# 64x128 array tiles with a row tile per token group, in place of 64x64 tiles with copied operands, in a convolution and feed-forward kernel

## Chip, cores, metric

One core of one Trainium2 chip. The metric is device time in microseconds of a whole execution. Every kernel was run several times next to the kernel before on the same chip. Engines: PE is TensorE (PEld its weight loads), ACT ScalarE, DVE VectorE, POOL GpSimd, SP the queue that issues most transfers.

## The reference

A causal convolution of 7 taps along the sequence, with one softmax-normalised set of taps for each of 8 heads, feeds a two-layer network with an ELU between the layers:

```python
# x (8, 4096, 192), weight (8, 7), w_in (192, 2048), w_out (2048, 192)
w = softmax(weight)                                   # per head
a[b, s, h*24 + g] = sum_k w[h, k] * x[b, s + k - 6, h*24 + g]
h = a @ w_in                                          # 32768 tokens
g = where(h > 0, h, exp(min(h, 0)) - 1)
out = g @ w_out                                       # (32768, 192) f32
```

## The kernel before

Work goes in 32 *supersteps* of 1,024 tokens, each of two groups of 512. A superstep has 16 *pairs*; a pair makes 128 of the 2,048 features for all its tokens:

- PE: H = w_in^T a, contracted in three chunks of 64 rows. The chunks are 64 rows so that two row tiles of the array can work at once (in the trace the four matmuls of a round start within about 10 ns).
- ACT takes exp of H (two instructions of 128x512), POOL clamps it, DVE combines it with H to g (written as `gT`).
- H lives in a ring of three PSUM slots; a slot is free again when DVE has read it. A convolution takes a slot of the same ring.
- PE: the output matmuls ("rounds") of an earlier superstep stand between the H blocks.

```python
LAG = -4                                   # output of superstep t starts 4 pairs before its last H
HALF_STEPS = (10, 9, 9, 9, 9, 9, 9)        # output rounds behind each H block, 64 per half
CONV_AT = ((7, 2, 0), (15, 2, 1))          # pair, supersteps ahead, group
X_AT = (1, 5, 13)                          # pairs at which POOL issues loads of x
...
# H: four 64x64 tiles at once, r = row tile (a feature block of 64), c = token group
for j in range(3):
    for r in range(2):
        f = 2 * q + r
        for c in range(2):
            pe.matmul(H[HP*c : HP*(c+1), k % 3, GS*r : GS*(r+1)],
                      w_in[HP*r : HP*(r+1), j, HP*f : HP*(f+1)],
                      att[HP*r : HP*(r+1), s % 2, j, c, :],      # att and w_in stand twice, in
                      tile_position=(HP*r, HP*c), ...)           # partitions 0-63 and 64-127
...
# output: g = row tile and token group, c = half of a block of 128 tokens
for r in range(r0, r1):
    f, kb = divmod(r, 2) if half == 0 else divmod(r, NF)[::-1]
    W(s_tt, 2 * NQ * t + f + 1)
    for g in range(2):
        for c in range(2):
            t0 = P * b + HP * c
            pe.matmul(ops[HP*c : HP*(c+1), g, D*kb : D*(kb+1)],
                      gT[HP*g : HP*(g+1), t % NG3, f, t0 : t0+HP],
                      w_out[HP*g : HP*(g+1), f, :],              # w_out stands twice too
                      tile_position=(HP*g, HP*c), ...)
```

## Time and profile before

| kernel before | |
|---|---|
| time, median of 4 | 850.47 us (847.81 to 851.45) |
| first H matmul / first output round | 34.45 / 55.95 us |
| superstep, mean | 25.1 us |
| PE instructions | 25,088 matmuls and as many weight loads |

The superstep in this document is the mean distance, in the trace, between ACT's copies of every second output half (30 distances, from the first half of superstep 0 to that of superstep 30).

The queues of the transfers, from the same page: name and kind, packets, MB, share of 16 engines.

```profile
q1 hardware_dynamic: 68016, 69.30, 26.1%
q0 software_dynamic: 40944, 15.72, 17.1%
q8 instruction: 196, 3.21, 1.6%
```

The page gives the queue q8 as one of instructions. 3.21 MB over 2 x 25,088 PE instructions are 64 bytes each, so I take this queue for PE's own stream; all its 196 packets have 16,384 bytes, which is 256 instructions.

PE in the timeline of the kernel before, around a convolution (start, length, engine, what, count, idle before):

```profile
386.12 0.84 PE L392 MATMUL H<-att,w_in 64*64 64x512 bf16 x12
386.79 0.91 PE L414 MATMUL ops<-w_out,gT 64*64 64x192 f16 x36
387.54 0.82 PE L392 MATMUL H<-att,w_in 64*64 64x512 bf16 x12
388.18 0.91 PE L414 MATMUL ops<-w_out,gT 64*64 64x192 f16 x36
389.24 0.67 PE L370 MATMUL H<-Tm,xg 128*24 128x24 bf16 x40
390.53 0.84 PE L392 MATMUL H<-att,w_in 64*64 64x512 bf16 x12 [0.62 <-DVE gT L333]
```

The last column shows the stall of the ring: H behind the convolution waits 0.62 us for DVE. Starts count here, not lengths, since matmuls overlap in the records (the H block at 387.54 has a length of 0.82 us, and the next rounds start within it): from 387.54 to 388.18 an H block takes 0.64 us, and from 386.79 to 387.54 nine rounds take 0.75 us.

### The profile page before, as it was taken

What the parts mean: (1) busy time and instruction counts of PE and PEld (TensorE: products, weight loads), DVE (VectorE), ACT (ScalarE), POOL (GpSimd) and SP (SyncE); (2) the same over time, 40 slices, a digit from 0 to 9 for tenths busy, and PEclk for the clock granted to TensorE, in tenths of its full rate; (3) what the DMA queues carried; (4) which work ended last, traced back from release to release, by engine and by line L of the source; (5) the groups of instructions that cost most, each with busy time, mean ns of one, the idle gap of its engine ahead of it and who ended that gap; (6) DMA issues with size and microseconds to landing.
All of it is one profiled execution on the core that took longest, in us unless ns stands there. A gap on an engine that the chain in (4) does not pass through costs nothing.

```text
span 849.9 us, 54707 instructions
## 1 busy us (share of the span) xinstructions
PE 752.5 (89%) x25088; PEld 560.4 (66%) x25088; DVE 643.3 (76%) x1031; ACT 650.5 (77%) x1156; POOL 662.8 (78%) x1115
## 2 busy tenths in 40 slices
PE   0279999889999999989999989999999999999997
PEld 0147667667766666766766766767766766677776
DVE  1277878777878878778777877878787887888894
ACT  1278888778878878878888868888787887888884
POOL 3378888778788788878788868788778878877883
PEclk9999999999999999999999999999999999999999
DMA  7774453444453444444335444344445434443211
GB/s 121 131 148 114 105 121 94 94 99 111 106 123 90 109 94 110 115 106 111 102 80 117 112 101 110 96 93 112 106 106 122 100 91 103 111 115 94 91 41 59
DMA packets 109190, 88.51 MB, mean 104 GB/s; under 512 B 46432, under 2 KB 95584, under 8 KB 108896
## 3 DMA queue, kind: packets, MB, share of 16 engines
q1 hardware_dynamic: 68016, 69.30, 26.1%
q0 software_dynamic: 40944, 15.72, 17.1%
q8 instruction: 196, 3.21, 1.6%
q14 instruction: 34, 0.28, 0.1%
HBM read 56.89 MB, written 42.24 MB: 117 GB/s over the span
## 4 chain that ended last, share of the span: by engine, by line
PE 35%; POOL 26%; DVE 17%; ACT 9%; issue 9%; DMA 3%; SPq 0%; POOLq 0%; ACTq 0%
POOL E L248 20%; PE H L392 19%; DVE gT L333 17%; PE ops L414 16%; ACT E L294 6%; POOL xg L198 5%; ACT osb L271 3%; DMA conv_slots<-csb 1%; DMA conv_band<-wprb 1%; DMA att<-conv_slots 1%; PE H L370 1%; DMA Tm<-conv_band 0%; SPq L475 0%; DMA wq<-in_weight_dram 0%; ACT csb L283 0%
## 5 line engine op out<-in xcount | busy, mean ns | idle before, releaser
L333 DVE SCALAR_TENSOR_TENSOR gT<-E,H 128x512 f16<-128x512 f32 x1024 | 640.0, 682 | 191.0 <-POOL E L248 182.1
L248 POOL TENSOR_SCALAR E<-E 128x512 f32<-128x512 f32 x1024 | 602.4, 614 | 148.1 <-ACT E L294 142.7
L294 ACT ACTIVATE E<-H 128x512 f32<-128x512 f32 x1024 | 546.6, 605 | 138.4 <-PE H L392 138.1
L392 PE MATMUL H<-att,w_in 64*64 64x512 bf16 x6144 | 429.7, 381 | 57.7 <-DVE gT L333 38.3
L414 PEld LDWEIGHTS ops<-w_out,gT 64*64 64x64 f16 x16384 | 377.9, 107 | 90.1 <-issue 9.5
L414 PE MATMUL ops<-w_out,gT 64*64 64x192 f16 x16384 | 422.5, 243 | 7.5 <-issue 6.4
L392 PEld LDWEIGHTS H<-att,w_in 64*64 64x64 bf16 x6144 | 165.9, 107 | 154.2 <-DVE gT L333 63.5
L283 ACT ACTIVATE csb<-H 128x1024 bf16<-128x1024 f32 x64 | 65.5, 1024 | 47.1 <-PE H L370 47.1
L370 PE MATMUL H<-Tm,xg 128*24 128x122 bf16 (+1 forms) x2560 | 43.2, 212 | 28.3 <-DMA Tm<-conv_band 15.2
L370 PEld LDWEIGHTS H<-Tm,xg 128*24 128x24 bf16 x2560 | 33.9, 93 | 41.2 <-DMA Tm<-conv_band 15.2
L198 POOL DMA_DIRECT2D xg<-in_x_dram x64 | 53.0, 830 | 10.2 <-DMA Tm<-conv_band 10.2
L271 ACT ACTIVATE osb<-ops 128x768 f32<-128x768 f32 x64 | 52.3, 817 | 8.4 <-PE ops L414 8.4
L235 POOL DMA_DIRECT2D w_out<-in_moe_w_out_dram x1 | 1.1, 1102 | 15.4 <-DMA att<-conv_slots 15.4
L207 POOL DMA_DIRECT2D xg<-in_x_dram x8 | 4.8, 604 | 0.3 <-issue 0.3
L217 POOL DMA_DIRECT2D w_in<-in_moe_w_in_dram x6 | 3.5, 606 | 0.3 <-PE H L370 0.3
L206 POOL MEMSET xg<- 6x192 bf16 x8 | 2.0, 247 | 0.3 <-POOLq L512 0.3
L326 DVE MEMSET H<- 128x2048 f32 x1 | 1.8, 1765 | 0.4 <-issue 0.4
L307 DVE TENSOR_REDUCE wmx<-wq 128x8 f32<-128x56 f32 x1 | 0.2, 213 | 2.2 <-DMA wq<-in_weight_dram 2.2
L260 ACT ACT_TABLE_LOAD x1 | 1.3, 1283 | 0.7 <-PEq L512 0.7
L264 ACT ACTIVATE wex<-wq 128x56 f32<-128x56 f32 x1 | 0.2, 249 | 1.7 <-DVE wq L309 1.7
L305 DVE MEMSET Tm<- 128x544 uint32 x1 | 0.5, 512 | 0.9 <-PEq L512 0.9
L316 DVE TENSOR_REDUCE wsum<-wex 128x8 f32<-128x56 f32 x1 | 0.2, 211 | 0.3 <-ACT wex L264 0.3
(9 smaller groups left out, 1.5 us busy)
## 6 DMA issues: line engine op xcount, KB each, us to landing
att<-conv_slots SPq DMA_DIRECT2D x192, 128.0 KB
out_dram<-osb SPq DMA_DIRECT2D x128, 192.0 KB, 3.3
conv_slots<-csb SPq DMA_DIRECT2D x64, 256.0 KB, 2.2
xg<-in_x_dram POOLq DMA_DIRECT2D x40, 192.0 KB, 3.7
xg<-in_x_dram POOLq DMA_DIRECT2D x24, 240.0 KB, 5.3
w_in<-in_moe_w_in_dram POOLq DMA_DIRECT2D x6, 128.0 KB, 5.6
w_in<-w_in SPq DMA_DIRECT2D x2, 384.0 KB, 5.3
w_out<-in_moe_w_out_dram POOLq DMA_DIRECT2D x1, 768.0 KB, 8.4
```

Of the source, the lines that this page charges most:

```text
L198: g.dma_start(xg[:, s % NXB, w0:w1, :], src).then_inc(s_x[s % NXB], 16)
L206: g.memset(xg[0:PAD, b, 0, :], 0.0).then_inc(s_z)
L207: g.dma_start(xg[PAD:P, b, 0, :], x_flat[t0 : t0 + P - PAD, :]).then_inc(s_x[b], 16)
L217: g.dma_start(w_in[0:HP, j, FH * k : FH * (k + 1)], bass.AP(tensor=moe_w_in.tensor, offset=8 * j * FF + FH * k, ap=[[CPH * FF, HEADS], [FF ...
L248: g.tensor_scalar(out=E[:, n % NE, u, :], in0=E[:, n % NE, u, :], scalar1=1.0, scalar2=0.0, op0=ALU.min, op1=ALU.max,).then_inc(s_clp)
L271: a.activation(osb[:, b, :, :, :].rearrange("p g k d -> p g (k d)"), ops[:, :, 0 : 2 * D], ACT.Copy,).then_inc(s_oev)
L283: a.activation(csb[:, m % 4, :, :], H[:, slot_of_conv[m] % 3, :].rearrange("p (b t) -> p b t", b=2), ACT.Copy,).then_inc(s_ce)
L294: a.activation(E[:, n % NE, u, :], H[:, k, GS * u : GS * (u + 1)], ACT.Exp).then_inc(s_exp)
L333: v.scalar_tensor_tensor(out=gT[:, s % NG3, 2 * q + u, :], in0=E[:, n % NE, u, :], scalar=1.0, in1=H[:, slot_of_pair[n] % 3, GS * u : GS * ...
L370: ins = pe.matmul(H[SLOT * q : SLOT * q + CPH, k % 3, GS * hb + o : GS * hb + o + nc_], xg[:, s % NXB, w, CPH * h : CPH * (h + 1)], Tm[:, ...
L392: ins = pe.matmul(H[HP * c : HP * (c + 1), k % 3, GS * r : GS * (r + 1)], w_in[HP * r : HP * (r + 1), j, HP * f : HP * (f + 1)], att[HP * ...
L414: ins = pe.matmul(ops[HP * c : HP * (c + 1), g, D * kb : D * (kb + 1)], gT[HP * g : HP * (g + 1), t % NG3, f, t0 : t0 + HP], w_out[HP * g ...
```

## The change

The intent: tiles of 64 rows and 128 columns. Row tile r works on token group r, so the convolution's output needs no second copy in the other 64 partitions, and w_out needs none either. In the output, the two tiles swap token groups after half of the rounds, so that by design they never accumulate into the same token group's half of `ops` at the same time. PE gets half the matmuls, each twice as wide. The order of work changes with it.

```diff
-LAG = -4
-HALF_STEPS = (10, 9, 9, 9, 9, 9, 9)
-CONV_AT = ((7, 2, 0), (15, 2, 1))
-X_AT = (1, 5, 13)
+LAG = -1
+WARM = (20, 18)                            # dummy matmuls ahead of the convolution and of H
+HALF_STEPS = (9, 9, 7, 7, 11, 11, 10)
+CONV_AT = ((4, 2, 0), (12, 2, 1))
+X_AT = ((4, 1), (12, 2), (13, 0))          # pair, part
 ...
-            order.append(("o",) + rounds_at[n])
-        for at, ahead, g in CONV_AT: ...    # convolution behind the output step
+            mid = (r0 + r1) // 2 if convs else r1
+            order.append(("o", t, half, r0, mid))
+            for k, g in convs:
+                conv_at(k, g)               # convolution in the middle of the output step
+            if mid < r1:
+                order.append(("o", t, half, mid, r1))
 ...
-                            f = 2 * q + r
-                            for c in range(2):
-                                ins = pe.matmul(H[HP*c : HP*(c+1), k % 3, GS*r : GS*(r+1)], ...
-                                    tile_position=(HP * r, HP * c))
+                            ins = pe.matmul(H[:, k % 3, GS*r : GS*(r+1)],
+                                w_in[HP*r : HP*(r+1), j, FC*q : FC*(q+1)],
+                                att[HP*r : HP*(r+1), s % 2, j, :], ...
+                                tile_position=(HP * r, 0))
 ...
+                        second, (q, kb) = r // (NR // 2), divmod(r % (NR // 2), 2)
+                        if second:
+                            W(s_swap, 2 * (2 * t + half + 1))
-                        for g in range(2):
-                            for c in range(2): ...            # four 64x64 tiles
+                        for rt in range(2):
+                            g = rt ^ second
+                            ins = pe.matmul(ops[:, g, D*kb : D*(kb+1)],
+                                gT[HP*rt : HP*(rt+1), t % NG3, q, g, t0 : t0 + P],
+                                w_out[HP*rt : HP*(rt+1), q, :], ...
+                                tile_position=(HP * rt, 0))
```

(Cut: layouts of `att`, `gT` and `w_out`; the start-up, where w_in is loaded later, attention reads start per group on two queues, and loads of x and w_out move between the first pairs.)

More of the change, by code (lines that the diff above doesn't have):

```diff
@@ L14 @@
 HP = 64
+FC = 128
 D = 192
@@ L28 @@
 NG3 = 2
-LAG = -4
-HALF_STEPS = (10, 9, 9, 9, 9, 9, 9)
-CONV_AT = ((7, 2, 0), (15, 2, 1))
-X_AT = (1, 5, 13)
+LAG = -1
+QA = 10
+WARM = (20, 18)
+HALF_STEPS = (9, 9, 7, 7, 11, 11, 10)
+CONV_AT = ((4, 2, 0), (12, 2, 1))
+EARLY_CONV = {5: (1, 0), 7: (1, 1), 11: (2, 0), 14: (2, 1)}
 XW = 5
+X_AT = ((4, 1), (12, 2), (13, 0))
+EARLY_LOADS = ((1, 1, 1), (2, 1, 2), (4, "w_out", 0), (6, 2, 1), (7, 2, 2), (13, 3, 1), (15, 3, 2))
 PIECES = (
@@ L58, in bass_lightweight_conv__then__act_elu_kernel @@
     assert S % SUP == 0 and tuple(out.shape) == (NT, D)
-    NF = FF // HP
-    NQ = NF // 2
+    NQ = FF // FC
+    NR = 4 * NQ
     assert NQ == 16
@@ L63, in bass_lightweight_conv__then__act_elu_kernel @@
     SPB = S // SUP
-    assert SPB >= NXB
     NP = NS * NQ
+    assert SPB > NXB
     x_flat = x.rearrange("b s d -> (b s) d")
@@ L96, in bass_lightweight_conv__then__act_elu_kernel @@
                 r += cnt
-            assert r == 2 * NF
+            assert r == NR
     for n in range(NP + NQ + LAG):
@@ L102, in bass_lightweight_conv__then__act_elu_kernel @@
             order.append(("h", n))
-        if n in rounds_at:
-            order.append(("o",) + rounds_at[n])
-        for at, ahead, g in CONV_AT:
-            if i == at and s + ahead < NS and n < NP:
-                conv_at(s + ahead, g)
-        if n in (3, 5) and NS > 1:
-            conv_at(1, (3, 5).index(n))
+        if s == 0:
+            convs = [EARLY_CONV[n]] if n in EARLY_CONV else []
+        else:
+            convs = [(s + ahead, g) for at, ahead, g in CONV_AT if at == i and n < NP]
+        convs = [(k, g) for k, g in convs if k < NS]
+        if n in rounds_at:
+            t, half, r0, r1 = rounds_at[n]
+            mid = (r0 + r1) // 2 if convs else r1
[4 more added lines that the diff above has]
+                order.append(("o", t, half, mid, r1))
+        else:
+            for k, g in convs:
+                conv_at(k, g)
     band = nc.dram_tensor("conv_band", (P, HEADS, TW), BF16).ap()
@@ L127, in bass_lightweight_conv__then__act_elu_kernel @@
         csb = sbuf("csb", [P, 4, 2, GS], BF16)
-        att = sbuf("att", [P, 2, 3, 2, GS], BF16)
+        att = sbuf("att", [P, 2, 3, GS], BF16)
         w_in = sbuf("w_in", [P, 3, FF], BF16)
-        w_out = sbuf("w_out", [P, NF, D], FP16)
+        w_out = sbuf("w_out", [P, NQ, D], FP16)
         E = sbuf("E", [P, NE, 2, GS], FP32)
-        gT = sbuf("gT", [P, NG3, NF, GS], FP16)
+        gT = sbuf("gT", [P, NG3, NQ, 2, GS], FP16)
         osb = sbuf("osb", [P, 2, 2, 2, D], FP32)
@@ L140, in bass_lightweight_conv__then__act_elu_kernel @@
         wprb = sbuf("wprb", [P, HEADS, KSIZE], BF16)
+        zw = sbuf("zw", [P, GS], BF16)
         scr = sbuf("scr", [P, 2], FP32)
@@ L152, in bass_lightweight_conv__then__act_elu_kernel @@
         s_z = sema("s_z")
+        s_zw = sema("s_zw")
         s_h = sema("s_h")
@@ L159, in bass_lightweight_conv__then__act_elu_kernel @@
         s_dw = [sema(f"s_dw{i}") for i in range(4)]
-        s_wd = [sema(f"s_wd{i}") for i in range(3)]
+        s_wd = [sema(f"s_wd{i}") for i in range(2)]
         s_tz = sema("s_tz")
@@ L164, in bass_lightweight_conv__then__act_elu_kernel @@
         s_mm2 = sema("s_mm2")
+        s_swap = sema("s_swap")
         s_oev = sema("s_oev")
@@ L178, in __call__ @@
                     self.eng.wait_ge(sem, value)
-        FH = FF // 2
+        WCOLS = ((0, P * QA), (P * QA, FF))
         NDMA_ATT = 6
@@ L186, in bass_lightweight_conv__then__act_elu_kernel, with read_att @@
             x_need[s] = (x_count[s % NXB], z_count)
+        def read_att(eng, W, s, g):
+            m = 2 * s + g
+            W(s_dw[m % 4], 16 * (m // 4 + 1))
+            for j in range(3):
+                src = bass.AP(
+                    tensor=bounce.tensor,
+                    offset=(2 * P * (s % 2) + 8 * j) * SUP + GS * g,
+                    ap=[[SLOT * SUP, HEADS], [SUP, 8], [1, GS]],
+                )
+                eng.dma_start(
+                    att[HP * g : HP * (g + 1), s % 2, j, :], src
+                ).then_inc(s_att[s % 2], 16)
         @block.gpsimd
@@ L190, in _gpsimd, with load_x @@
             W = Waits(g)
-            def x_windows(s, w0, w1, row):
+            def load_x(s, part):
+                b, t0 = s % NXB, s * SUP
+                first = s % SPB == 0
+                if part == 0 and not first:
+                    return
+                if s >= NXB:
+                    W(s_cv, 2 * (s - NXB) + 2)
+                if part == 0:
+                    g.memset(xg[0:PAD, b, 0, :], 0.0).then_inc(s_z)
+                    g.dma_start(
+                        xg[PAD:P, b, 0, :], x_flat[t0 : t0 + P - PAD, :]
+                    ).then_inc(s_x[b], 16)
+                    return
+                if part == 1:
+                    w0, w1, row = int(first), XW, t0 - PAD + CW * first
+                else:
+                    w0, w1, row = XW, NWIN, t0 + SUP - P - CW * (NWIN - 1 - XW)
                 src = bass.AP(
@@ L197, in x_windows @@
                 )
-                g.dma_start(xg[:, s % NXB, w0:w1, :], src).then_inc(s_x[s % NXB], 16)
-            def load_x(s, part):
-                b, t0 = s % NXB, s * SUP
-                first = s % SPB == 0
-                if s >= NXB:
-                    W(s_cv, 2 * (s - NXB) + 2)
-                if part == 0 and first:
-                    g.memset(xg[0:PAD, b, 0, :], 0.0).then_inc(s_z)
-                    g.dma_start(
-                        xg[PAD:P, b, 0, :], x_flat[t0 : t0 + P - PAD, :]
-                    ).then_inc(s_x[b], 16)
-                elif part == 1:
-                    x_windows(s, int(first), XW, t0 - PAD + CW * first)
-                elif part == 2:
-                    x_windows(s, XW, NWIN, t0 + SUP - P - CW * (NWIN - 1 - XW))
+                g.dma_start(xg[:, b, w0:w1, :], src).then_inc(s_x[b], 16)
             def load_w_in(k):
+                c0, c1 = WCOLS[k]
                 for j in range(3):
                     g.dma_start(
-                        w_in[0:HP, j, FH * k : FH * (k + 1)],
+                        w_in[0:HP, j, c0:c1],
                         bass.AP(
                             tensor=moe_w_in.tensor,
-                            offset=8 * j * FF + FH * k,
-                            ap=[[CPH * FF, HEADS], [FF, 8], [1, FH]],
+                            offset=8 * j * FF + c0,
+                            ap=[[CPH * FF, HEADS], [FF, 8], [1, c1 - c0]],
                         ),
@@ L227, in _gpsimd @@
                 load_x(0, part)
+            W(s_band, 32)
             load_w_in(0)
-            W(s_band, 48)
-            for part in range(3):
-                load_x(1, part)
-            W(s_cv, 2)
+            W(s_att[0], 16 * NDMA_ATT)
             load_w_in(1)
-            W(s_att[0], 16 * NDMA_ATT)
-            g.dma_start(
-                w_out[0:HP, :, :],
-                moe_w_out.rearrange("(f p) d -> p f d", p=HP),
-            ).then_inc(s_w[2], 16)
-            for s in range(2, min(NXB, NS)):
-                for part in range(3):
-                    load_x(s, part)
             for n in range(NP):
                 s, i = divmod(n, NQ)
-                if i in X_AT and s + NXB < NS:
-                    load_x(s + NXB, X_AT.index(i))
+                for at, what, part in EARLY_LOADS:
+                    if at != n:
+                        continue
+                    if what == "w_out":
+                        g.dma_start(
+                            w_out[:, :, :], moe_w_out.rearrange("(q p) d -> p q d", p=FC)
+                        ).then_inc(s_w[2], 16)
+                    elif what < NS:
+                        load_x(what, part)
+                for at, part in X_AT:
+                    if at == i and s >= 1 and s + NXB < NS:
+                        load_x(s + NXB, part)
                 for u in range(2):
@@ L287, in _scalar @@
                     ).then_inc(s_ce)
+                    if m == 1:
+                        read_att(a, W, 0, 0)
                 elif item[0] == "h":
@@ L298, in _scalar @@
                     _, t, half, r0, r1 = item
-                    if r1 == 2 * NF:
+                    if r1 == NR:
                         evac(2 * t + half)
@@ L304, in _vector @@
             W = Waits(v)
+            v.memset(zw[:], 0.0).then_inc(s_zw)
             v.memset(Tm[:], 0.0).then_inc(s_tz)
@@ L333, in _vector @@
                     v.scalar_tensor_tensor(
-                        out=gT[:, s % NG3, 2 * q + u, :],
+                        out=gT[:, s % NG3, q, u, :],
                         in0=E[:, n % NE, u, :],
@@ L353, in wait_slot, with warm @@
                     W(s_ce, was[1] + 1)
+            def warm(count):
+                W(s_zw, 1)
+                for _ in range(count):
+                    pe.matmul(ops[:, 0, :], zw[:, 0:P], zw[:], start=True, stop=True)
+            warm(WARM[0])
             for item in order:
@@ L382, in _tensor @@
                     s, q = divmod(n, NQ)
-                    W(s_w[q // 8], 48)
-                    W(s_wd[q // 8], 16)
+                    if n == 0:
+                        warm(WARM[1])
+                    W(s_w[q // QA], 48)
+                    W(s_wd[q // QA], 16)
                     W(s_att[s % 2], 16 * NDMA_ATT * (s // 2 + 1))
@@ L389, in _tensor @@
                         for r in range(2):
-                            f = 2 * q + r
-                            for c in range(2):
-                                ins = pe.matmul(
-                                    H[HP * c : HP * (c + 1), k % 3, GS * r : GS * (r + 1)],
-                                    w_in[HP * r : HP * (r + 1), j, HP * f : HP * (f + 1)],
-                                    att[HP * r : HP * (r + 1), s % 2, j, c, :],
-                                    start=(j == 0),
-                                    stop=(j == 2),
-                                    tile_position=(HP * r, HP * c),
-                                )
+                            ins = pe.matmul(
+                                H[:, k % 3, GS * r : GS * (r + 1)],
+                                w_in[HP * r : HP * (r + 1), j, FC * q : FC * (q + 1)],
+                                att[HP * r : HP * (r + 1), s % 2, j, :],
+                                start=(j == 0),
+                                stop=(j == 2),
+                                tile_position=(HP * r, 0),
+                            )
                     ins.then_inc(s_h)
@@ L403, in _tensor @@
                     W(s_w[2], 16)
-                    W(s_wd[2], 16)
                     if r0 == 0:
@@ L407, in _tensor @@
                     for r in range(r0, r1):
-                        f, kb = divmod(r, 2) if half == 0 else divmod(r, NF)[::-1]
-                        W(s_tt, 2 * NQ * t + f + 1)
-                        b = 2 * half + kb
-                        for g in range(2):
-                            for c in range(2):
-                                t0 = P * b + HP * c
-                                ins = pe.matmul(
-                                    ops[HP * c : HP * (c + 1), g, D * kb : D * (kb + 1)],
-                                    gT[HP * g : HP * (g + 1), t % NG3, f, t0 : t0 + HP],
-                                    w_out[HP * g : HP * (g + 1), f, :],
-                                    start=(r == 0 if half == 0 else f == 0),
-                                    stop=(r == 2 * NF - 1 if half == 0 else f == NF - 1),
-                                    tile_position=(HP * g, HP * c),
-                                )
-                    if r1 == 2 * NF:
+                        second, (q, kb) = r // (NR // 2), divmod(r % (NR // 2), 2)
+                        W(s_tt, 2 * (NQ * t + q) + 2)
+                        if second:
+                            W(s_swap, 2 * (2 * t + half + 1))
+                        t0 = 2 * P * half + P * kb
+                        for rt in range(2):
+                            g = rt ^ second
+                            ins = pe.matmul(
+                                ops[:, g, D * kb : D * (kb + 1)],
+                                gT[HP * rt : HP * (rt + 1), t % NG3, q, g, t0 : t0 + P],
+                                w_out[HP * rt : HP * (rt + 1), q, :],
+                                start=(r == 0),
+                                stop=(r == NR - 1),
+                                tile_position=(HP * rt, 0),
+                            )
+                            if r == NR // 2 - 1:
+                                ins.then_inc(s_swap)
+                    if r1 == NR:
                         ins.then_inc(s_mm2)
@@ L445, in copy_w @@
             def copy_w(k):
-                W(s_w[k], 16 if k == 2 else 48)
-                t = w_out if k == 2 else w_in[:, :, FH * k : FH * (k + 1)]
-                sy.dma_start(t[HP:P, :, :], t[0:HP, :, :]).then_inc(s_wd[k], 16)
+                W(s_w[k], 48)
+                c0, c1 = WCOLS[k]
+                sy.dma_start(w_in[HP:P, :, c0:c1], w_in[0:HP, :, c0:c1]).then_inc(s_wd[k], 16)
             copy_w(0)
@@ L455, in _sync @@
                     W(s_ce, m + 1)
-                    if s >= 2:
-                        W(s_att[s % 2], 16 * NDMA_ATT * (s // 2))
                     sy.dma_start(
@@ L461, in _sync @@
                     ).then_inc(s_dw[m % 4], 16)
-                    if g == 0:
-                        continue
-                    for k in range(m - 1, m + 1):
-                        W(s_dw[k % 4], 16 * (k // 4 + 1))
-                    if s >= 2:
-                        W(s_h, NQ * (s - 1))
-                    for j in range(3):
-                        src = bass.AP(
-                            tensor=bounce.tensor,
-                            offset=(2 * P * (s % 2) + 8 * j) * SUP,
-                            ap=[[SLOT * SUP, HEADS], [SUP, 8], [1, SUP]],
-                        )
-                        for r in range(2):
-                            sy.dma_start(
-                                att[HP * r : HP * (r + 1), s % 2, j, :, :].rearrange(
-                                    "p g t -> p (g t)"
-                                ),
-                                src,
-                            ).then_inc(s_att[s % 2], 16)
-                    if s == 0:
-                        copy_w(1)
-                        copy_w(2)
+                    if s == 0 and g == 1:
+                        read_att(sy, W, 0, 1)
+                        copy_w(1)
+                    elif s == 1:
+                        read_att(sy, W, 1, g)
+                elif item[0] == "h":
+                    s, i = divmod(item[1], NQ)
+                    if i == 1 and s >= 1 and s + 1 < NS:
+                        W(s_h, NQ * s)
+                        for g in range(2):
+                            read_att(sy, W, s + 1, g)
                 elif item[0] == "o":
                     _, t, half, r0, r1 = item
-                    if r1 < 2 * NF:
+                    if r1 < NR:
                         continue
```

## The prediction

> **What bounds the kernel now.** No engine is full: the page gives PE 89%, POOL 78%, ACT 77%, DVE 76%; the chain of waits is shared by PE 35%, POOL 26%, DVE 17%, ACT 9%. In the timeline one superstep (1,024 tokens, 16 pairs) repeats every 25.2 us (383.61 to 408.83). An undisturbed pair takes 1.39 us: 0.65 us for twelve H matmuls (three rounds of four array tiles, 216 ns each) and 0.74 us for nine output rounds of 82.5 ns. Per superstep PE's streams need 16 x 0.65 + 128 x 0.0825 + two convolutions of 0.65 = about 22.3 us. The other 2.9 us are stalls at the ring of three H banks: a bank is held about 3.4 us (matmul, two exps, POOL, DVE), longer when ACT's 1.02 us convolution copy, its 0.82 us output copy, or POOL's 0.8 us x-load issue comes between. They show as H matmuls and convolutions waiting for DVE gT (0.15 to 0.6 us each). The head is costly too: first H matmul at 34.4 us, first output round at 55.9 us.
>
> **What the change does to PE.** Half as many matmuls and weight loads, each 128 columns wide, two at once instead of four. Array time stays. [...] fewer instructions buy nothing by themselves. Weight loads get wider[...]. In the trace the second 64-column load into one tile starts 29 ns after the first, all four tiles loading side by side[...]. The swap wait has an H block between its halves and should cost nothing.
>
> **What pays.** (1) Steady state: the convolution goes into the middle of an 11-round output step, x-load issues beside it, output shares become uneven; ACT's copy falls into a longer gap between H blocks. Counting along the ring I expect 1.5 us of stalls per superstep instead of 2.9: 23.8 us. Attention reads halve (128 to 64 KB each), off the critical path. (2) Head: w_in is loaded only after the band's diagonal landed, attention reads start per group, on two queues, at half size; no w_out copy. Of the chain (band 12 us, Tm 3.2, convolution 2, slots write 7.3, attention read 5 to 9) the last two shrink: first H near 25 us, 9 us earlier. Dummy matmuls warm the clock (first H matmuls took 631 ns against 400 later; granted clock 0.92 in that window[...]). Output starts three pairs later in the order: first output round about 48 us. From the last superstep's first output round to the end, 18.8 us becomes about 16.5.
>
> **Sum.** 48 + 31 x 23.8 + 16.5 = 802 us, 5.6% faster; range 780 to 828. Chances: faster 0.88, same 0.08, slower 0.04.
>
> **What would show it.** Superstep 23 to 24.5; 18 output matmuls in about 0.75 us; H blocks 0.65; [...] H waits for DVE gT halved; first H before 28 us; DMA bytes down by about 13 MB; DVE, ACT and POOL busy times unchanged.
>
> **What would make it wrong.** [...] If the stalls come from ACT, POOL and DVE jitter and not from where the convolution stands, the time is near 838. If nearly all stalls vanish: 765.

What the trace of the kernel before shows is 82.5 ns for an output round of 192 columns and 216 ns for an H round of 512, 0.43 and 0.42 ns a column.

## More of the kernel before

From the page of the kernel before: busy time by engine, the chain that ended last, and the largest groups (line, engine, operation, tiles, shapes, count, busy us, mean ns, idle before and what ended it).

```profile
PE 752.5 (89%) x25088; PEld 560.4 (66%) x25088; DVE 643.3 (76%) x1031; ACT 650.5 (77%) x1156; POOL 662.8 (78%) x1115
...
PE 35%; POOL 26%; DVE 17%; ACT 9%; issue 9%; DMA 3%; SPq 0%; POOLq 0%; ACTq 0%
...
L333 DVE SCALAR_TENSOR_TENSOR gT<-E,H 128x512 f16<-128x512 f32 x1024 | 640.0, 682 | 191.0 <-POOL E L248 182.1
...
L392 PE MATMUL H<-att,w_in 64*64 64x512 bf16 x6144 | 429.7, 381 | 57.7 <-DVE gT L333 38.3
L414 PEld LDWEIGHTS ops<-w_out,gT 64*64 64x64 f16 x16384 | 377.9, 107 | 90.1 <-issue 9.5
L414 PE MATMUL ops<-w_out,gT 64*64 64x192 f16 x16384 | 422.5, 243 | 7.5 <-issue 6.4
```

No engine is full and the chain runs through four of them, so I read it as a ring, not an engine, that sets the pace. The two rows of output matmuls look harmless. The word "issue" in them (9.5 us for the weight loads, 6.4 us for the matmuls) is a wait that no semaphore explains.

## The result

The kernel after takes 786.24 us (median of 4, 785.85 to 787.84) against 850.47 us: ratio 0.9253, 95% interval 0.9228 to 0.9278. A ratio is the mean time of one kernel's fast runs over that of the other's fast runs of the same rounds, so it is not quite the ratio of the medians.

The same lines of the page of the kernel after:

```profile
PE 749.1 (96%) x13862; PEld 514.3 (66%) x13862; DVE 633.9 (81%) x1032; ACT 651.3 (83%) x1156; POOL 665.1 (85%) x1115
...
PE 47%; POOL 32%; ACT 7%; DVE 6%; issue 4%; DMA 3%; SPq 0%; DVEq 0%
...
L370 DVE SCALAR_TENSOR_TENSOR gT<-E,H 128x512 f16<-128x512 f32 x1024 | 630.3, 681 | 132.5 <-POOL E L282 132.3
...
L435 PE MATMUL H<-att,w_in 64*128 64x512 bf16 x3072 | 409.6, 380 | 19.6 <-DVE gT L370 9.1
L458 PE MATMUL ops<-w_out,gT 64*128 64x192 f16 x8192 | 420.0, 243 | 1.9 <-ACT osb L305 0.9
L458 PEld LDWEIGHTS ops<-w_out,gT 64*128 64x128 f16 x8192 | 347.6, 94 | 111.0 <-ACT osb L305 2.7
```

PE's busy time is nearly the same (749 against 752 us, of a span that is 66 us shorter), with half the instructions. Array time was not cut; the idle time between was. Two entries matter later: the weight load of 128 columns takes *less* time than the one of 64 did (94 against 107 ns), and "issue" is gone from the output matmuls.

Its queues:

```profile
q1 hardware_dynamic: 67720, 55.73, 22.5%
q0 software_dynamic: 40944, 15.72, 18.9%
q8 instruction: 108, 1.77, 0.9%
```

And PE around a convolution:

```profile
396.75 0.58 PE L458 MATMUL ops<-w_out,gT 64*128 64x192 f16 x10
397.25 0.66 PE L413 MATMUL H<-Tm,xg 128*24 128x24 bf16 x40
397.85 0.67 PE L458 MATMUL ops<-w_out,gT 64*128 64x192 f16 x12
398.35 0.81 PE L435 MATMUL H<-att,w_in 64*128 64x512 bf16 x6
399.00 0.99 PE L458 MATMUL ops<-w_out,gT 64*128 64x192 f16 x20
```

No wait is left here. The superstep is 22.96 us. Against the sum of the prediction:

| term | before | predicted | after |
|---|---|---|---|
| up to the first output round | 55.95 | 48 | 55.90 us |
| one superstep, first output rounds of supersteps 0 and 31 | 25.0 | 23.8 | 22.93 us |
| last superstep's first output round to the end | 18.8 | 16.5 | 17.4 us |
| 1st + 31 x 2nd + 3rd | 850 | 802 | 784 us |

The total fell within the range, but that it lies only 2% off is partly luck, since two errors of opposite sign went into it: 8 us too little for the head, 27 us (31 x 0.87) too much for the supersteps. So the experiments ask what made the supersteps faster than the schedule was expected to.

### The profile page after: what moved, and what is told of

It is laid out like the page before. It is cut to its first block, busy times and chain, and to the rows that moved or that the text cites. A ratio compares the mean times of both kernels' runs of the same rounds, so it can differ in the third digit from the quotient of the medians.

```text
span 784.1 us, 32200 instructions
## 1 busy us (share of the span) xinstructions
PE 749.1 (96%) x13862; PEld 514.3 (66%) x13862; DVE 633.9 (81%) x1032; ACT 651.3 (83%) x1156; POOL 665.1 (85%) x1115
## 4 chain that ended last, share of the span: by engine, by line
PE 47%; POOL 32%; ACT 7%; DVE 6%; issue 4%; DMA 3%; SPq 0%; DVEq 0%
POOL E L282 28%; PE H L435 24%; PE ops L458 21%; DVE gT L370 6%; ACT E L330 4%; ACT osb L305 3%; POOL xg L246 3%; PE H L413 2%; DMA xg<-in_x_dram 1%; DMA w_in<-in_moe_w_in_dram 1%; DMA conv_slots<-csb 1%; DMA conv_band<-wprb 1%; DMA att<-conv_slots 0%; DMA wq<-in_weight_dram 0%; SPq L216 0%
## 5 line engine op out<-in xcount | busy, mean ns | idle before, releaser
L370 DVE SCALAR_TENSOR_TENSOR gT<-E,H 128x512 f16<-128x512 f32 x1024 | 630.3, 681 | 132.5 <-POOL E L282 132.3
L435 PE MATMUL H<-att,w_in 64*128 64x512 bf16 x3072 | 409.6, 380 | 19.6 <-DVE gT L370 9.1
L458 PE MATMUL ops<-w_out,gT 64*128 64x192 f16 x8192 | 420.0, 243 | 1.9 <-ACT osb L305 0.9
L458 PEld LDWEIGHTS ops<-w_out,gT 64*128 64x128 f16 x8192 | 347.6, 94 | 111.0 <-ACT osb L305 2.7
L435 PEld LDWEIGHTS H<-att,w_in 64*128 64x128 bf16 x3072 | 132.3, 94 | 127.0 <-DVE gT L370 39.3
L395 PE MATMUL ops<-zw 128*128 128x512 bf16 x38 | 11.0, 455 | 1.2 <-DVE zw L341 1.2
L395 PEld LDWEIGHTS ops<-zw 128*128 128x128 bf16 x38 | 4.1, 113 | 7.3 <-issue 3.5
```

Of the source, the lines that this page charges most:

```text
L370: v.scalar_tensor_tensor(out=gT[:, s % NG3, q, u, :], in0=E[:, n % NE, u, :], scalar=1.0, in1=H[:, slot_of_pair[n] % 3, GS * u : GS * (u + ...
L395: pe.matmul(ops[:, 0, :], zw[:, 0:P], zw[:], start=True, stop=True)
L435: ins = pe.matmul(H[:, k % 3, GS * r : GS * (r + 1)], w_in[HP * r : HP * (r + 1), j, FC * q : FC * (q + 1)], att[HP * r : HP * (r + 1), s ...
L458: ins = pe.matmul(ops[:, g, D * kb : D * (kb + 1)], gT[HP * rt : HP * (rt + 1), t % NG3, q, g, t0 : t0 + P], w_out[HP * rt : HP * (rt + 1) ...
```

## The experiments

An overview first. "Stalls" are pauses of PE in mid-stream after the first 60 us: more than 0.45 us from one matmul's start to the next one's, both of the same source line, counted up to 18 us before the last matmul. The rate is matmuls and weight loads per us between 70 and 770 us. Both were worked out from the records in the trace. In the kernel before, 7 of the 16 are no shortage of instructions (see the last part). "M" is PE's matmuls.

| run | M | median us | ratio to before (95%) | superstep us | PE instr./us | stalls, us |
|---|---|---|---|---|---|---|
| before | 25,088 | 850.47 | | 25.09 | 62.2 | 16, 16.8 |
| e1_sched | 25,088 | 836.57 | 0.9754 (0.9656 to 0.9851) | 24.33 | 64.2 | 37, 33.9 |
| e4_split | 25,126 | 819.69 | 0.9579 (0.9525 to 0.9632) | 24.10 | 64.8 | 46, 34.6 |
| f1_both_half | 25,126 | 816.44 | 0.9576 (0.9544 to 0.9608) | 24.07 | 64.8 | 34, 24.9 |
| f2_out_half | 22,054 | 792.19 | 0.9285 (0.9257 to 0.9312) | 23.11 | 59.2 | 0 |
| f3_h_half | 16,934 | 789.02 | 0.9252 (0.9225 to 0.9279) | 23.03 | 45.5 | 0 |
| after | 13,862 | 786.24 | 0.9253 (0.9228 to 0.9278) | 22.96 | 37.2 | 0 |

The kernel before was at 850.47 to 855.65 us on the chips; only the ratios compare. All results were correct.

The row of f1_both_half comes from a profile of 817.2 us, as do the lines shown of this run. The profile that was kept of it is another execution (812.8 us) and gives 23.83 us a superstep, 65.5 instructions per us and 21 stalls of 15.3 us: how much PE stands still varies from one execution to the next, the argument below does not. The kept profile of f2_out_half, too, is another one: 23.10 us, 59.2 per us, no stall.

### e1_sched: the schedule alone

```diff
 # in the kernel before: 64x64 tiles, both copies and the old start-up kept
-LAG = -4; HALF_STEPS = (10, 9, 9, 9, 9, 9, 9); CONV_AT = ((7, 2, 0), (15, 2, 1)); X_AT = (1, 5, 13)
+LAG = -1; HALF_STEPS = (9, 9, 7, 7, 11, 11, 10); CONV_AT = ((4, 2, 0), (12, 2, 1)); X_AT = ((4, 1), (12, 2), (13, 0))
+# and the convolution in the middle of its output step
```

> The kernel before, 64x64 tiles and both copies kept, with the schedule of the kernel after alone: output lag of one pair, output shares 9,9,7,7,11,11,10, the convolution in the middle of an output step, x loads at pairs 4, 12 and 13. My theory, that the steady state was won by the schedule: superstep near 23.1 us as in the kernel after (25.2 in the kernel before), first output round a little after 60 us because the old head stays, so 785 to 800 us, ratio to before 0.925 to 0.945. Rival, that the tile shape wins (half the instructions, wider loads, half the attention reads): superstep stays at 24.5 or more, time 835 to 855.

Measured: 836.57 us, ratio 0.9754; formally unclear, since the interval crosses 2%, and one of its four runs (842.38 us) was put down as slow (without it the median is 834.1 us). Its superstep was 24.33 us, not 23.1. My theory that the schedule won the supersteps had foretold 0.925 to 0.945, and fell here; the rival's 24.5 us was not met either, but it was nearer, and the time lies in its 835 to 855 us. Where the time went, PE in its timeline shows:

```profile
415.24 0.84 PE L403 MATMUL H<-att,w_in 64*64 64x512 bf16 x12
415.91 0.33 PE L425 MATMUL ops<-w_out,gT 64*64 64x192 f16 x5
416.53 0.85 PE L425 MATMUL ops<-w_out,gT 64*64 64x192 f16 x31 [0.29 <-issue]
```

A step of 9 rounds (36 matmuls) breaks off after 5 matmuls and goes on half a microsecond later, in the middle of an accumulation, with nothing to wait for.

### e4_split: the tile shape alone

```diff
 # in the kernel after: each H and output matmul in two of 64x64, all else kept
-    ops[:, g, ...], gT[HP*rt : HP*(rt+1), t % NG3, q, g, t0 : t0 + P], tile_position=(HP*rt, 0)
+    for c in range(2):
+        tc = t0 + HP * c
+        ops[HP*c : HP*(c+1), g, ...], gT[HP*rt : HP*(rt+1), t % NG3, q, g, tc : tc + HP], tile_position=(HP*rt, HP*c)
```

> The kernel after with every H and output matmul cut into two of 64x64 tiles, everything else kept (schedule, layout, swap, head). My theory: array time and thus the kernel unchanged, 782 to 792 us, 18 rounds' worth of output still 82.5 ns a round, weight loads 107 ns each again in the table against 94. Rival, tile shape wins: 820 to 850 us.

Measured: 819.69 us, ratio 0.9579; the weight loads took 107 ns again. This is 3.3% of the kernel before away from the kernel after, though every round still takes 82.5 ns (median 82 to 83 ns in both traces). My theory fell a second time. PE in the timeline of this run:

```profile
404.63 0.82 PE L437 MATMUL H<-att,w_in 64*64 64x512 bf16 x12
405.28 0.50 PE L462 MATMUL ops<-w_out,gT 64*64 64x192 f16 x15
406.57 0.65 PE L462 MATMUL ops<-w_out,gT 64*64 64x192 f16 x21 [0.80 <-issue]
407.01 0.86 PE L437 MATMUL H<-att,w_in 64*64 64x512 bf16 x12
```

It has 46 such stalls, 34.6 us in all. The supersteps cost 31 x (24.10 - 22.96) = 35 us more than in the kernel after, so the stalls are about the whole difference. The transfer records tell what came before their ends: each of the 46 ended 1.22 to 1.58 us after a 16 KB packet of queue q8 had landed. For random times in that stretch the share would be 10%. I read it so: PE had run out of instructions.

The place of the stalls in PE's stream says the same. Count PE's records in the trace by their start (matmuls, weight loads and some 70 semaphore records): 45 of the 46 stalls begin at record 192 of a block of 256, the other one at 191. In e1_sched all 37 begin at record 193, in the kept profile of f1_both_half all 21, and in the kernel before 9 of 16. A cause that knew nothing of the blocks would not pick one place in 256.

### f1_both_half, f2_out_half, f3_h_half: count against shape

e4_split changes shape and count together. These three keep the 64x128 tiles and cut the matmuls along the moving side instead, so only the count grows.

```diff
 # f1: both; f2: the output only; f3: H only
-    H[:, k % 3, GS*r : GS*(r+1)] ... att[..., :]                  # moving 512
+    for nh in range(2): H[..., GS*r + 256*nh : ...] ... att[..., 256*nh : 256*(nh+1)]
-    ops[:, g, D*kb : D*(kb+1)] ... w_out[..., :]                  # moving 192
+    for nh in range(2): ops[..., D*kb + 96*nh : ...] ... w_out[..., 96*nh : 96*(nh+1)]
```

> The kernel after with its 64x128 tiles kept, but every H and output matmul cut in two along the moving side (512 into 256+256, 192 into 96+96), so that PE gets as many instructions as with 64x64 tiles (25,126 matmuls). The first four runs overthrew my theory that the tile shape is neutral: with 64x64 tiles the kernel after took 819.7 us, and PE stood still 46 times in the middle of a stream, 34.6 us in all, each time to resume 1.2 to 1.6 us after a 16 KB packet of the instruction queue had landed. New theory, PE's instructions arrive too late: such stalls appear here too, 40 to 50 of them with the same 1.2 to 1.6 us, 30 to 40 us in all, and with some 10 us for the extra matmuls' fixed cost the time is 820 to 840 us; if 128-column loads don't hide in 42 ns the rounds get longer, the demand falls, and the time is longer still, with fewer such stalls. Rival, the 64x64 shape (column tiles) itself is at fault: no such stalls, 786 to 800 us.

Measured: 816.44 us, ratio 0.9576, the same as the 64x64 tiles of e4_split. There are 34 stalls, 24.9 us; 33 of them ended 1.25 to 1.6 us after a packet's landing (in the kept profile 21 of 21, after 1.21 to 1.61 us). That is fewer and shorter than the 40 to 50 stalls and 30 to 40 us that I expected. But each round now takes 2 x 42.5 ns instead of 82.5 ns, 10 us over 4,096 rounds (what the expectation calls the extra matmuls' fixed cost), and 24.9 + 10 is again the 35 us. (In the kept profile it is 15.3 + 10 against 31 x (23.83 - 22.96) = 27 us.) One of the stalls:

```profile
138.93 0.72 PE L462 MATMUL ops<-w_out,gT 64*128 64x96 f16 x26
140.57 0.39 PE L462 MATMUL ops<-w_out,gT 64*128 64x96 f16 x10 [0.93 <-issue]
```

So in these kernels the shape of the tiles does not make the stalls; the number of instructions does.

> As the last, but only the output matmuls cut in two (22,054 matmuls). Instruction theory: the demand that is too high is the one of the output rounds, 8 instructions in 82 ns, so most of the stalls stay: 25 to 45 of them, 20 to 35 us, time 810 to 835 us. Rival: no such stalls, 786 to 800 us.

Measured: 792.19 us, ratio 0.9285, and no stall at all. Here I missed: in its output rounds this kernel asks for instructions as fast as f1 does, and I had taken that density for the cause. I take it that the mean rate over longer stretches counts. 59.2 instructions per us are supplied without a stall, and the three kernels that want more all end up at 64 to 66 per us. The packets say the same. In before, e1_sched, e4_split and f1_both_half their shortest distances (5th percentile) are all 3.4 us and the mean in the last three is 3.9 to 4.0 us, that is 256 / 3.94 = 65 instructions per us; in f2_out_half the mean is 4.3 us and in the kernel after 6.9 us.

> As the last but one, but only the H matmuls cut in two (16,934 matmuls): 24 instructions in 650 ns, below the demand of the uncut output rounds. Instruction theory: no stalls in mid-stream, 785 to 795 us. If the sheer number of matmuls costs, whatever their density: 795 to 805 us.

Measured: 789.02 us, ratio 0.9252, no stall. As expected.

### e2_conv_end, e3_even, g1_shift: which part of the schedule matters

With instructions out of the way, the parts of the schedule can be undone in the kernel after.

```diff
 # e2_conv_end
-            mid = (r0 + r1) // 2 if convs else r1
+            mid = r1
 # e3_even
-HALF_STEPS = (9, 9, 7, 7, 11, 11, 10)
+HALF_STEPS = (10, 9, 9, 9, 9, 9, 9)
 # g1_shift
-HALF_STEPS = (9, 9, 7, 7, 11, 11, 10)
+HALF_STEPS = (10, 11, 11, 8, 8, 8, 8)
```

> The kernel after with the convolution behind the whole output step and not in its middle. My theory (ACT's 1.02 us copy needs the gap): stalls of H on DVE gT come back around each convolution, 0.3 to 0.6 us each, superstep 23.7 to 24.2, time 800 to 825 us. If its place within the step does not matter: 782 to 790 us.

Measured: 794.07 us, ratio 0.9291 (0.9251 to 0.9330), superstep 23.21 us. This lies between the two ranges of the expectation, nearer to the second. The convolution's place within its step is worth 0.25 us a superstep, under half of the least that I expected (two stalls of 0.3 us). The two ratios' intervals overlap, so the 0.4% is not firm; I rely on the superstep, 0.25 us longer, where the traces of the kernel after and of e6 to e9 agree within 22.96 to 22.98 us.

> The kernel after with even output shares 10,9,9,9,9,9,9, so that the swap falls within a step (after 4 of its rounds) and no H block stands between its halves. My theory: each swap then shows a drain of 0.2 to 0.3 us, 64 swaps, 13 to 19 us, and the conv steps of 9 rounds add some 0.2 us of stall each, so 800 to 820 us. If neither the shares nor the swap matter: 782 to 790 us.

Measured: 822.14 us, ratio 0.9621 (0.9580 to 0.9662), slightly over what I expected. In the table of waits (between 60 and 800 us) both suspects appear:

```profile
PEld H L435 <- DVE gT L370: 40.0, 64, 0.8
PE H L435 <- DVE gT L370: 24.8, 56, 0.5
PEld ops L458 <- PE ops L458: 19.6, 62, 0.3
```

The third line is the swap inside a step, PE waiting for its own output matmuls: 62 times, at most 0.3 us each, 19.6 us in all. The first two are the ring.

> The kernel after with output shares 10,11,11,8,8,8,8: the swap again falls between two steps, as in the kernel after, but the convolution stands in a step of 8 rounds and not of 11. It divides the 36 us that even shares cost. If that was the swap inside a step: no PE wait on its own outputs, 786 to 795 us. If it was the short gap around the convolution and before the pair without output: H waits for DVE gT of 0.4 us and more stay, 805 to 822 us.

Measured: 818.52 us, ratio 0.9590 (0.9564 to 0.9616). The swap again falls between steps, and its wait is gone; the waits of the ring grew instead:

```profile
PEld H L435 <- DVE gT L370: 60.9, 119, 0.8
PE H L435 <- DVE gT L370: 29.7, 56, 0.6
```

The two kernels differ by 0.3% with overlapping intervals, although 19.6 us of swap waits are gone. What the swap inside a step costs by itself is not shown: g1_shift also has shorter steps around the convolution (8 rounds, against 9 in e3_even), and the ring's waits grew there. What is shown is that the shares matter. The order of the kernel after, with steps of 11 rounds right before and around the convolution, is worth 0.9590 - 0.9253 = 3.4% of the kernel before against that of g1_shift, more than any other part of the schedule tested. That it is ACT's extra 1.02 us copy that needs the longer gap fits the H blocks' waits for DVE, but no run isolates it.

### e6_nowarm, e7_longwarm, e8_x1_early, e9_head: the start

```diff
 # e6_nowarm            # e7_longwarm            # e9_head
-WARM = (20, 18)        -WARM = (20, 18)         -WARM = (20, 18)
+WARM = (0, 0)          +WARM = (20, 56)         +WARM = (20, 62)    # and the lines of e8
 # e8_x1_early
+            load_x(1, 1); load_x(1, 2)          # at about 12 us, before POOL waits for the attention reads; cut from EARLY_LOADS
             W(s_att[0], 16 * NDMA_ATT)
```

> The kernel after without its 38 dummy matmuls. In the trace of the kernel after the granted clock was back at 0.5 from 22.0 us on, 4.9 us before the first H matmul, which took 583 to 631 ns, so the dummies did not warm the H matmuls. Theory: they save at most the cold part of the first convolutions, 785 to 788 us without them. If my prediction's claim that they help the head holds: 789 to 793 us.

Measured: 786.99 us, ratio 0.9224 (0.9194 to 0.9255). The 38 dummy matmuls bring nothing. In the trace of the kernel after, the dummies end at 18.6 us, the granted clock falls to 0.5 at 22.0 us and the first H matmul starts at 26.9 us. The fall came 3.4 us after the last dummy, and the clock stayed at 0.5 until 32.3 us. Nor had the first two convolutions gained: together they took 1.91 us in the kernel before, without dummies, and 1.91 us in the kernel after.

> The kernel after with 56 dummy matmuls instead of 18 ahead of the first H matmul, so that PE is kept busy up to the landing of the attention reads at 26.8 us. Theory: the clock is then at 1.0 when H starts, the first H matmuls take 376 to 400 ns instead of 583 to 631, the first output round comes 1.5 to 3 us earlier than 55.9, 782 to 785 us. If the clock does not set the pace of the first pairs: 785 to 788 us, first output round at 55 to 56 us.

Measured: 787.87 us, ratio 0.9234 (0.9209 to 0.9258). The first H matmuls do run at full clock (373 to 376 ns; 18 of them in 2.12 us, where the first 24 of the kernel after took 5.58 us), but they started 0.9 us later, and from the third pair on the ring sets the pace. PE in its timeline:

```profile
27.82 2.12 PE L435 MATMUL H<-att,w_in 64*128 64x512 bf16 x18 [0.86 <-DMA att<-conv_slots]
31.73 0.82 PE L435 MATMUL H<-att,w_in 64*128 64x512 bf16 x6 [1.79 <-DVE gT L370]
33.82 0.82 PE L435 MATMUL H<-att,w_in 64*128 64x512 bf16 x6 [1.26 <-DVE gT L370]
35.80 1.46 PE L435 MATMUL H<-att,w_in 64*128 64x512 bf16 x6 [1.16 <-DVE gT L370]
```

PE waits for DVE 1 to 2 us per pair here, and at 35.8 us the clock drops again: the pair that starts then takes 1.46 us instead of 0.82. The first output round came at 57.8 us, no earlier. The second theory of the expectation (the clock does not set the pace) holds in its reason and its time, 785 to 788 us, not in its first output round, 55 to 56 us.

> The kernel after with the two x loads of superstep 1 issued at about 12 us, before POOL's wait for the attention reads, and not between the first pairs. Theory: POOL's 0.94 and 0.81 us issues and the 1.6 us wait of the third convolution for x leave the first pairs, 2 to 3 us; but the loads [...] put the first H matmul off by 1 to 3 us; sum within 2 us of the kernel after, 784 to 788 us. If POOL's issues set the pace of the head: 780 to 783 us.

Measured: 786.80 us, ratio 0.9217 (0.9192 to 0.9242). First H at 28.3 us, 1.4 us later, and pairs 3 to 5 only 1.2 to 1.3 us apart instead of 2.0; first output round at 56.4 us. Gain and loss cancel, as expected.

> The last two together: x of superstep 1 loaded early and 62 dummy matmuls ahead of the first H matmul. Alone, each put the first H matmul off by about 1 to 1.4 us (27.8 and 28.3 us against 26.9) and gained about as much or less after it. Together: H starts near 28.3 with a warm clock and no x-load issue between its pairs, pairs 1 to 5 come 0.65 to 1.3 us apart, first output round at 53.5 to 55 us, so 783 to 786 us, a ratio of 0.918 to 0.922 to the kernel before. If nothing but the ring of banks sets the pace: 786 to 788 us.

Measured: ratio 0.9194 (0.9172 to 0.9217), median 787.17 us (784.86 to 788.29) on a chip where the kernel before took 855.65 us. The first output round came at 54.3 us. The ratio is within my expectation, the median is not, as this chip's runs were all longer. By ratio it is the fastest kernel, 0.6% under the kernel after. But e6_nowarm and e8_x1_early, no faster in us than the kernel after, also came out at 0.9224 and 0.9217 on their chips, so a gain in total time is not shown. What the trace shows is a first output round 1.6 us earlier at the same superstep (22.98 us).

## Why the prediction was right or wrong

- *"fewer instructions buy nothing by themselves"* is the step that failed, though the total was within its range. It looked at the array alone: a round took 82.5 ns with four matmuls, and it takes 82.5 ns with two. True, and beside the point. PE is also a consumer of instructions. As I read the stalls, with 50,000 of them the supply held the superstep at 24.1 us or more: in e4_split and f1_both_half, whose schedules were good enough for 23 us, the stalls fill the rest (34.6 of 35 us, and 24.9 us with 10 us of longer rounds). Halving the count brought 819.69 to 786.24 us. The clue stood in the profile before, as "issue" waits of the output matmuls; 9 of the 16 mid-stream stalls of the kernel before, 10.7 of 16.8 us, bear the signature of 1.2 to 1.6 us after a landing, and the same nine begin at the same record of a block; the other seven are waits of H for DVE. What fewer instructions would buy under the old schedule was not measured.
- *"23.8 us"* per superstep was mis-sized because of it. The schedule alone gave 24.33 us (e1_sched), the schedule and half the instructions 22.96 us. Neither half gets far alone: the schedule with the old count stops at the supply, and half the count with other shares (e3_even, g1_shift) stops at the ring, both near 0.96. From the kernel before, in this order: schedule 2.5%, new layout and head 1.8%, tile width 3.3% of the kernel before (ratios 0.9754, 0.9579, 0.9253). The first part is the least firm, 1.5 to 3.4% by its interval. In another order the parts would get other sizes.
- *"ACT's copy falls into a longer gap between H blocks"* was right as far as the shares of the output steps go: undone in g1_shift they cost 3.4%. ACT's copy as the reason was not isolated. That the convolution stands in the middle of its step is the smaller part (e2_conv_end).
- *"first H near 25 us"* came out at 26.9 us, about right; *"first output round about 48 us"* at 55.9 us, wrong by 8 us. I had counted 15 pairs at about 1.5 us. They took 1.9 us each. PE in the timeline of the kernel after:

```profile
26.88 5.58 PE L435 MATMUL H<-att,w_in 64*128 64x512 bf16 x24 [8.25 <-DMA att<-conv_slots]
33.19 0.82 PE L435 MATMUL H<-att,w_in 64*128 64x512 bf16 x6 [0.73 <-DVE gT L370]
35.17 1.00 PE L435 MATMUL H<-att,w_in 64*128 64x512 bf16 x6 [1.16 <-DVE gT L370]
37.78 1.04 PE L413 MATMUL H<-Tm,xg 128*24 128x122 bf16 x40 [1.61 <-DMA xg<-in_x_dram]
```

  The first four pairs (24 matmuls) run at half clock (granted 0.5 from 22.0 to 32.3 us; most of these matmuls took 631 ns, against 376 later), the next two wait for the ring, the convolution waits for an x load that the change itself had moved between the pairs. Mending two of these causes (e9_head) brought 1.6 us. What holds the rest of the first superstep was not tested.
- *"Dummy matmuls warm the clock"* was wrong for these 38: they end at 18.6 us, 8 us before the first H matmuls, which took 583 to 632 ns in the kernel after (see e6_nowarm). With 56 ahead of H it came true, 373 to 376 ns, but the clock is not what the pairs wait for (e7_longwarm).
- *"Weight loads get wider"*, and what they would cost, was the worry. The table shows 94 ns for a load of 128 columns, less than the 107 ns for 64, and smaller than I had expected. The rounds still take 82.5 ns, and in f1_both_half each half of one takes 42.5 ns beside loads of 94 ns, so the loads overlap the matmuls. Why the wider load is the shorter one was not shown.
- *"The swap wait [...] should cost nothing"*: right. With an H block between, "PE ops" hardly appears among the waits of the kernel after (0.6 us before weight loads, in two waits).
- The other signs came true: transfers fell from 88.5 to 73.7 MB; DVE, ACT and POOL busy times stayed within 2%; H waits of PEld for DVE gT fell from 63.5 to 39.3 us, by 38% and not by half. The tail came to 17.4 us, not 16.5, as the last superstep's swap waits 1.1 us for DVE there.

Open: why the stalls begin at the same record of a block; why packets come 3.4 us apart at least, and whether other transfers slow them; and half the instructions with the *old* schedule, which I could not build, since with a lag of four pairs the swap would wait for features that are not yet made.

## What to carry to other kernels

Count the instructions of an engine, not only their time: here 59.2 matmuls and weight loads per us ran without a stall, while kernels at 62 to 66 per us had stalls of up to 34.6 us in 819, and 13,862 matmuls of twice the width in place of 25,126 brought 819.69 to 786.24 us, though no round got shorter. Look for pauses in the middle of an accumulation that no semaphore explains, and compare them with the landings of the instruction queue's packets. And expect two limits that lie close together to hide one another: undo each part of a change from the finished kernel too, not only add it to the old one.
